# Fetching the first two tables of the second block's short transform one step earlier in the program

## The chip, the cores and the metric

The kernel runs on one core of a Trainium2 chip. The metric is the device time of one execution in microseconds (us). Beside it stands the profile of one execution: every instruction of the five engines (PE for matrix products, ACT for exponentials, DVE for element-wise work, POOL, which here mostly issues transfers, and SP, which issues the other transfers), and the transfers themselves.

## The reference

Two unrelated results are put side by side: an attention layer with 32 query heads and one shared key and value head, and a long causal convolution.

```python
# half A: x is (1, 2048, 512), 32 heads of 16, one key and one value head
q = (x @ wq).reshape(B, S, 32, 16).transpose(0, 2, 1, 3)
k, v = x @ wk, x @ wv
p = softmax(einsum("bhqd,bkd->bhqk", q, k) * 16 ** -0.5)
a = einsum("bhqk,bkd->bhqd", p, v).transpose(0, 2, 1, 3).reshape(B, S, 512) @ wo

# half B: q, k, v are (1, 2048, 512)
k_shift = sum(shift(k, i) * shift_k[:, i] for i in range(4))   # four taps along the sequence
kv = k_shift * v
y = irfft(rfft(pad(kv)) * rfft(pad(ssm_k)))[:2048] + kv * ssm_D
b = q * y

out = concatenate([a, b], axis=-1)                             # (1, 2048, 1024)
```

## The kernel before

**Attention is the backbone.** The scores of 16 stacks of queries against 16 tiles of keys are computed tile by tile. For each tile PE makes 8 products into a pair of PSUM banks (`keys`, L1092), ACT takes the exponential of 128 x 1024 elements (`exp`, L1110), and PE multiplies the result with the values (`pv`, L1134). The scores have two such bank pairs, so the scores of a tile wait for the exponential of the tile two before.

**The convolution fills what is left.** Half B is done in two blocks of 256 channels, as transforms made of products with tables of cosines and sines (PE, `halves`, L274) and a 16-point transform on DVE. A block has these parts:

- the *short* transform (`short_forward`): the element-wise product `a` of the four taps and `v`, for 128 x 2 x 256 elements in each of eight groups (`m2` = 0 to 7), is multiplied with the table `ff` of its group;
- the *long* transform (`long_forward`): the same with the convolution's kernel;
- the product of the two spectra and the inverse 16-point transform, both on DVE;
- the *inverse* transform (`backward`): eight groups, each with a table `fi` and a slice of `q`; DVE multiplies the outcome with `q` into `r` (L490), and POOL sends `r` to the output (L492).

**Tables.** `table` (L316 to L320) allocates one of four rotating buffers (tag `ft`) for a table of 128 x 2 x 2 x 128 numbers and issues two transfers of 128 KB for it on POOL's queue. The `ff` and the `fi` tables share these four buffers. `short_forward` fetches the tables of its groups 0 and 1 when it begins, and the table of group `m2 + 1` in each later step. `paced` makes a transfer wait for the exponential that was issued two tiles before.

**Order.** The order of all instructions is fixed when the program is built. Python generators ("threads") stand for the parts; at each tile `_Fill.turn` asks each thread in turn for work and lets it emit as much as a budget allows. Each engine then runs what was emitted for it in that order, and waits at an instruction until the semaphores it needs are set. Two threads matter here. `conv_pe` runs, for the place of the change, `backward(0)` and then `short(1)`, which calls `short_forward(1, ...)`. `conv_short` runs `short_products(1, ...)`, which makes the `a` of the second block on DVE and issues, for each group, the transfers of the `kk` rows two groups ahead (L398) and of `v` (L411) on POOL. It may begin when `backward(0)` has reached its group 7, where `("b", 0)` is added to `self.seen`.

**POOL's queue is in order.** A transfer that waits there holds up every transfer behind it. Each transfer issued on POOL uses one of eight semaphores in turn (DMASW0 to DMASW7), and waits until the transfer that used the same one before, eight transfers earlier, has landed.

The first product of group 0 of the second block waits for its table's first transfer and for `a` of group 0:

```python
y = self.nc.tensor.matmul(out[j : j + 32, cols], w[r, j : j + 32], x[r], ...)   # L274, w is the table, x is a
```

Of the kernel before, what the change touches and what calls it, by code (L numbers as in the profile page):

```python
# [111 lines left out]
class _Emit:  # L112
# [203 lines left out]
    def table(self, n, m2):  # L316
# [2 lines left out]
            self.paced(self.nc.gpsimd.dma_start(t[:, i], self.I[n][:, 2 * m2 + i]))  # L319
        return t  # L320

    def s2(self, n, shape=(2, CB), dt=F32):
        return self.w.tile([P, *shape], dt, tag="s2", bufs=S2, name=self.nm(n))

# [109 lines left out]

    def short_forward(self, blk, cx):

        ft = {i: self.table("ff", i) for i in range(2)}
        for m2 in range(8):
            yield from self.after(("a", blk, m2))
            if 2 <= m2 + 1 < 8:  # L440
                ft[m2 + 1] = self.table("ff", m2 + 1)
            yield from self.forward(self.kv2[m2], cx, 2 * m2, ft[m2])
            self.seen.add(("x", blk, m2))
# [15 lines left out]
    def backward(self, blk):  # L459

        nc, w = self.nc, self.w
        cs = slice(blk * CB, (blk + 1) * CB)
        ft, q = {i: self.table("fi", i) for i in range(2)}, {}

        def load(m2):
            if m2 > 1:
                ft[m2] = self.table("fi", m2)
            q[m2] = self.s2("q")
            for i in range(2):
                self.paced(nc.gpsimd.dma_start(q[m2][:, i], self.qr[:, 2 * m2 + i, cs]))  # L470

        load(0)
        load(1)
        yield WAIT, 4
        yield from self.after(("y", blk))
        cx, (g1, g2) = self.sp["y", blk]
        for m2 in range(8):
            if m2 < 6:
                load(m2 + 2)
            if m2 == 7:  # L480
                self.seen.add(("b", blk))
            r = self.s2("r")
            cols, work = slice(0, CB), [[], []]
            for i in range(2):
                m = 2 * m2 + i
                for cc in range(2):
                    x = cx[:, cc, 4 * g2[m // 4] + g1[m % 4], :]
                    work[i].append((cols, ft[m2][:, i, cc, :], x))
            b = yield from self.halves(*work, 2, 850)
            nc.vector.tensor_tensor(r, self.both[:, :, cols], q[m2], ALU.mult)  # L490
            for i in range(2):
                nc.gpsimd.dma_start(self.orr[:, 2 * m2 + i, D + blk * CB : D + (blk + 1) * CB], r[:, i])  # L492
# [1153 lines left out]
```

## Time and profile before

| | |
|---|---|
| time, median of 3 runs | 983.58 us (983.55 to 984.63) |
| the profiled execution's own time | 983.59 us |
| its span, first to last instruction | 981.7 us |
| PE busy / ACT busy / DVE busy / POOL busy | 95% / 97% / 76% / 18% of the span |
| mean granted clock of PE | 0.998 |
| chain that ended last | PE 49%, ACT 35%, issue 7%, DVE 6%, DMA 2% |

The span is what the profile covers; the time has 1.89 us more around it. Busy shares are means over stages; the waits and the rows in order of time tell which engine holds up which at a place.

### The profile page before, as it was taken

The numbers are of one execution on the slowest core, as the hardware profiler recorded it, in microseconds if no ns is written. First come the engines' busy times: TensorE is split into PE (matmuls) and PEld (weight loads), VectorE is DVE, ScalarE is ACT, GpSimd is POOL, SyncE is SP. The second block draws the span as 40 slices with busy tenths as digits, with TensorE's granted clock in tenths as the row PEclk, the third lists the DMA queues.
The fourth block names the chain that finished last, engine by engine and source line by source line (L and its number), as shares of the span: only waits on it lengthen the run. The fifth ranks groups of instructions, "written<-read, shape, count | busy, mean of one in ns | idle before, by whom it ended". The sixth has DMA issues, their size and how long they took to land.

```text
span 981.7 us, 51442 instructions
## 1 busy us (share of the span) xinstructions
PE 934.5 (95%) x23570; PEld 462.4 (47%) x23570; DVE 748.9 (76%) x932; ACT 951.2 (97%) x1032; POOL 173.3 (18%) x321
## 2 busy tenths in 40 slices
PE   8999999989999999999899899999988999999996
PEld 5344454435444444444444455444434444444453
DVE  4647785988369989998996578799889927876753
ACT  5999999999999999999999999999999999999994
POOL 5240231321030001110533432000000132100000
PEclk9999999999999999999999999999999999999999
DMA  7252432431133212211443233011121232112101
GB/s 253 74 172 81 141 118 73 105 105 56 35 91 85 87 55 89 84 55 49 146 130 109 90 117 97 22 55 44 54 83 56 65 119 83 60 56 76 49 11 48
DMA packets 69205, 82.93 MB, mean 84 GB/s; under 512 B 20752, under 2 KB 58294, under 8 KB 68982
## 3 DMA queue, kind: packets, MB, share of 16 engines
q1 hardware_dynamic: 47558, 43.48, 14.1%
q0 software_dynamic: 20320, 35.46, 12.2%
q8 instruction: 186, 3.05, 1.3%
q10 hardware_dynamic: 1104, 0.64, 0.2%
q14 instruction: 37, 0.30, 0.1%
HBM read 54.46 MB, written 25.03 MB: 81 GB/s over the span
## 4 chain that ended last, share of the span: by engine, by line
PE 49%; ACT 35%; issue 7%; DVE 6%; DMA 2%; SPq 0%; POOL 0%; ACTq 0%; DVEq 0%
ACT p L1110 34%; PE f L1134 22%; PE s L1092 15%; PE f L274 10%; DVE sp L189 1%; DMA r<-rd 1%; DVE sp L193 1%; DMA xa<-in_A_x 1%; DVE sp L457 0%; DMA ff<-in_ff 0%; PE f L663 0%; DVE o L1278 0%; PE f L255 0%; PE f L693 0%; DVE ao L1143 0%
## 5 line engine op out<-in xcount | busy, mean ns | idle before, releaser
L1110 ACT ACTIVATE p<-s 128x1024 f32<-128x1024 f32 x1008 | 929.8, 1068 | 6.6 <-PE s L1092 5.1
L1134 PE MATMUL f<-p,vx 64*32 64x512 f32 (+1 forms) x8832 | 544.3, 552 | 0.4 <-ACT p L1110 0.2
L1092 PE MATMUL s<-st,kst 49*32 49x512 f16 x8128 | 422.5, 380 | 31.6 <-ACT p L1110 27.8
L1092 PEld LDWEIGHTS <-kst 49*32 49x32 f16 x8192 | 199.3, 89 | 395.3 <-issue 347.7
L1134 PEld LDWEIGHTS f<-p,vx 64*32 64x32 f32 x8832 | 175.0, 106 | 26.0 <-issue 3.0
L314 DVE COPY sp<-f 128x1024 f32<-128x1024 f32 x32 | 39.1, 1222 | 62.6 <-PE f L274 62.6
L189 DVE TENSOR_TENSOR sp<-sp 128x2048 f32<-128x2048 f32 x35 | 80.0, 2287 | 0.9
L319 POOL DMA_DIRECT2D ff<-in_ff x64 | 35.3, 557 | 235.3 <-ACT p L1110 216.9
L274 PE MATMUL f<-wo,o 64*32 64x512 f16 x1440 | 56.6, 375 | 0.9 <-DVE wp L1330 0.5
L1143 DVE COPY ao<-f 128x512 f32<-128x512 f32 (+1 forms) x33 | 22.2, 674 | 40.5 <-PE f L1134 40.2
L274 PE MATMUL f<-xT,wq 64*32 64x512 f16 x1344 | 51.0, 375 | 0.0
L319 POOL DMA_DIRECT2D fi<-in_fi x32 | 17.5, 552 | 176.5 <-ACT p L1110 176.3
L189 DVE TENSOR_TENSOR sp<-sp,sp 128x2048 f32<-128x2048 f32 x19 | 43.4, 2286 | 0.5
L274 PE MATMUL f<-a,ff 64*32 64x256 f32 x1024 | 41.2, 377 | 1.4 <-DMA ff<-in_ff 1.4
L274 PE MATMUL f<-hT,ff 64*32 64x256 f32 x1024 | 40.8, 377 | 0.7 <-DVE hT L368 0.7
L274 PE MATMUL f<-sp,fi 64*32 64x256 f32 x1024 | 39.9, 375 | 0.0
L492 POOL DMA_DIRECT2D out<-r x32 | 17.3, 546 | 123.8 <-DVE r L490 112.4
L429 DVE TENSOR_TENSOR a<-a,t 128x512 f32<-128x512 f32 x48 | 33.1, 690 | 1.5
L420 DVE TENSOR_TENSOR t<-kk,tpb 128x512 f32<-128x512 f32 (+1 forms) x50 | 33.0, 663 | 0.0
L347 POOL DMA_DIRECT2D hin<-in_B_ssm_k x32 | 21.1, 662 | 60.0 <-ACT p L1110 58.5
L193 DVE TENSOR_TENSOR sp<-sp 128x1024 f32<-128x1024 f32 x26 | 30.8, 1215 | 0.0
L490 DVE TENSOR_TENSOR r<-f,q 128x512 f32<-128x512 f32 x16 | 11.0, 688 | 25.4 <-PE f L274 25.3
(197 smaller groups left out, 788.3 us busy)
## 6 DMA issues: line engine op xcount, KB each, us to landing
ff<-in_ff POOLq DMA_DIRECT2D x64, 128.0 KB, 2.9
od<-ao SPq DMA_DIRECT2D x60, 128.0 KB
qd<-qp SPq DMA_DIRECT2D x48, 128.0 KB
st<-qd SPq DMA_DIRECT2D x62, 98.0 KB
kk<-in_B_k POOLq DMA_DIRECT2D x32, 128.0 KB, 2.8
v<-in_B_v POOLq DMA_DIRECT2D x32, 128.0 KB, 2.7
hin<-in_B_ssm_k POOLq DMA_DIRECT2D x32, 128.0 KB, 5.6
fi<-in_fi POOLq DMA_DIRECT2D x32, 128.0 KB, 2.9
```

What stands on the lines that cost most here:

```text
L189: v.tensor_tensor(out, a, b, op)
L193: v.tensor_tensor(part(out), part(a), part(b), op)
L274: y = self.nc.tensor.matmul(out[j : j + 32, cols], w[r, j : j + 32], x[r], start=half == m == 0, stop=half == 1 and m == k - 1,)
L314: self.nc.vector.tensor_copy(out, self.both.rearrange("p i (q n) -> p i q n", q=2))
L319: self.paced(self.nc.gpsimd.dma_start(t[:, i], self.I[n][:, 2 * m2 + i]))
L347: self.paced(nc.gpsimd.dma_start(dst, src))
L420: nc.vector.tensor_tensor(out[:, n], kk[:, x], tap(i, n.stop - n.start), ALU.mult)
L429: nc.vector.tensor_tensor(a, a, t, ALU.add)
L1092: self.nc.tensor.matmul(s[j : j + 32, e, :], (self.kst[k * P] if k * P in self.kst else self.kst[k * P - P][:, P:CB])[rows, j : j + 32], s ...
L1110: self.exps[u % 4] = self.nc.scalar.activation(self.pt[u], s, AF.Exp, scale=LN2 * DH**-0.5 / SC / SC)
L1134: nc.tensor.matmul(self.acc[e][32 * j : 32 * j + 32, m], vx[rows, :], y, start=k == 0, stop=stop)
L1143: nc.vector.tensor_copy(a, self.acc[0][:, m])
```

## The change

`backward`, when it reaches group 7 of block 0, now also allocates and fetches the tables of groups 0 and 1 of the second block's short transform, and `short_forward` of block 1 takes them from there. For block 0 nothing is changed.

```diff
+    def first_tables(self):
+        return {i: self.table("ff", i) for i in range(2)}
+
     def short_forward(self, blk, cx):
 
-        ft = {i: self.table("ff", i) for i in range(2)}
+        ft = self.next_ft if blk else self.first_tables()
         for m2 in range(8):
             yield from self.after(("a", blk, m2))
...
     def backward(self, blk):
...
             if m2 == 7:
                 self.seen.add(("b", blk))
+                self.next_ft = self.first_tables() if blk == 0 else None
             r = self.s2("r")
```

The order on POOL at the end of block 0's inverse transform, before the change. `out<-r` are the transfers of groups 5, 6 and 7 of `backward(0)` (the third is group 7's), `kk` and `v` are loads of the second block for DVE, and the two `ff` are the tables of groups 0 and 1:

```order
L492 DMA out<-r_12243 128x256 x2
L492 DMA out<-r_12437 128x256 x2
L398 DMA kk_10955<-in_B_k 128x256 x2
L411 DMA v_12673<-in_B_v 128x256 x2
L492 DMA out<-r_12670 128x256 x2
L319 DMA ff_12842<-in_ff 128x256 x2
L319 DMA ff_12845<-in_ff 128x256 x2
L398 DMA kk_10955<-in_B_k 128x256 x2
L411 DMA v_12904<-in_B_v 128x256 x2
```

The same place in the changed program (its line numbers are 3 or 4 higher from `first_tables` on):

```order
L496 DMA out<-r_12243 128x256 x2
L496 DMA out<-r_12437 128x256 x2
L319 DMA ff_12670<-in_ff 128x256 x2
L319 DMA ff_12673<-in_ff 128x256 x2
L401 DMA kk_10955<-in_B_k 128x256 x2
L414 DMA v_12679<-in_B_v 128x256 x2
L496 DMA out<-r_12676 128x256 x2
L401 DMA kk_10955<-in_B_k 128x256 x2
L414 DMA v_12904<-in_B_v 128x256 x2
```

The four table transfers moved ahead of six others: `kk` and `v` of group 0's step and the last `out<-r`. These are the only transfers on POOL that change places.

With their waits, the transfers behind group 6's `out<-r` were, before (`Activation` is the pacing exponential, `PE` the last reader of the buffer, DMASWn the transfer eight places earlier):

```order
L398 DMA kk_10955<-in_B_k 128x256 [waits DMASW6_49,Activation_49]
L398 DMA kk_10955<-in_B_k 128x256 [waits DMASW7_49]
L411 DMA v_12673<-in_B_v 128x256 [waits DMASW0_49]
L411 DMA v_12673<-in_B_v 128x256 [waits DMASW1_49]
L492 DMA out<-r_12670 128x256 [waits DMASW2_49,DVE_49]
```

and are now:

```order
L319 DMA ff_12670<-in_ff 128x256 [waits DMASW6_49,Activation_49]
L319 DMA ff_12670<-in_ff 128x256 [waits DMASW7_49]
L319 DMA ff_12673<-in_ff 128x256 [waits DMASW0_49,PE_49]
L319 DMA ff_12673<-in_ff 128x256 [waits DMASW1_49]
L401 DMA kk_10955<-in_B_k 128x256 [waits DMASW2_49]
L401 DMA kk_10955<-in_B_k 128x256 [waits DMASW3_49]
L414 DMA v_12679<-in_B_v 128x256 [waits DMASW4_49]
L414 DMA v_12679<-in_B_v 128x256 [waits DMASW5_49]
L496 DMA out<-r_12676 128x256 [waits DMASW6_49,DVE_49]
```

The wait for the pacing exponential moved from `kk` to the first `ff`, the second `ff` waits for PE's last reading of its buffer, and `v` now waits for the landing of group 6's `out<-r` (DMASW4 and DMASW5). On PE, ACT, DVE and SP every instruction stands where it stood.

## The prediction

> **What bounds the kernel now.** I read the page first, then the wait table, then the rows in order of time around the place of the change. From the page:
>
> ```profile
> span 981.7 us, 51442 instructions
> PE 934.5 (95%) x23570; PEld 462.4 (47%) x23570; DVE 748.9 (76%) x932; ACT 951.2 (97%) x1032; POOL 173.3 (18%) x321
> L1110 ACT ACTIVATE p<-s 128x1024 f32<-128x1024 f32 x1008 | 929.8, 1068 | 6.6 <-PE s L1092 5.1
> L274 PE MATMUL f<-a,ff 64*32 64x256 f32 x1024 | 41.2, 377 | 1.4 <-DMA ff<-in_ff 1.4
> ```
>
> ACT and PE are both full, and the exponentials of L1110 stood idle for only 6.6 us in all. The last row is the place of this change: in 1024 products with `ff` tables and data `a`, PE waited for a table once, for 1.4 us. The wait table for 552 to 562 us shows that this one wait reaches ACT:
>
> ```profile
> PE f L274 <- DMA ff<-in_ff: 1.4, 1, 1.4
> ACT p L1110 <- PE s L1092: 1.4, 1, 1.4
> DVE a L431 <- DMA v<-in_B_v: 0.7, 1, 0.7
> ```
>
> The chain of waits runs through the same transfer (start, length, what):
>
> ```profile
> 551.18 0.70 DVE r L490
> 552.17 0.47 POOL out L492
> 552.71 0.54 POOL out L492
> 553.24 4.17 DMA ff<-in_ff
> 557.54 0.67 PE f L274 x9
> ```
>
> So the table issued at 553.24 landed at 557.41 (553.24 + 4.17), and PE began with it at 557.54. It was issued late because POOL stood before it in group 7's `out<-r`, which waits for `r` of 551.18. ACT around it:
>
> ```profile
> 539.76 17.58 ACT L1110 ACTIVATE p<-s 128x1024 f32<-128x1024 f32 x19
> 558.75 185.11 ACT L1110 ACTIVATE p<-s 128x1024 f32<-128x1024 f32 x201 [1.41 <-PE s L1092]
> 559.82 1.94 ACT L1110 ACTIVATE p<-s 128x1024 f32<-128x1024 f32 x2
> ```
>
> Nineteen exponentials ran without a gap, then a gap of 1.41 us, then 201 without a gap: ACT is the limit on both sides of the hole.
>
> **The change, part by part.** *The hole that goes.* Of the 19 exponentials the last takes 1.07 us (the 1068 ns of the group), so the others follow each other every (17.58 - 1.07) / 18 = 0.917 us. The next would have begun at 539.76 + 19 x 0.917 = 557.19; it began at 558.75, 1.56 us late. The one after it began 1.07 us behind, at 559.82, another 0.15 us over the beat: 1.71 us late. The gap alone is 1.41 us. These are the lower and the upper bound, 1.41 and 1.71; I take **1.6 us**, between the 1.56 of the first exponential and the 1.71 that the second has lost.
>
> *Can PE fill it?* PE's rows:
>
> ```profile
> 545.48 0.41 PE L1092 MATMUL s<-st,kst 49*32 49x512 f16 x8
> 545.69 1.06 PE L1134 MATMUL f<-p,vx 64*32 64x512 f32 x16
> 547.31 0.41 PE L1092 MATMUL s<-st,kst 49*32 49x512 f16 x8
> 554.64 0.41 PE L1092 MATMUL s<-st,kst 49*32 49x512 f16 x8 [0.35 <-ACT p L1110]
> 555.72 0.41 PE L1092 MATMUL s<-st,kst 49*32 49x512 f16 x8
> 557.54 0.67 PE L274 MATMUL f<-a,ff 64*32 64x256 f32 x12 [1.41 <-DMA ff<-in_ff]
> ```
>
> Behind 8 score products the next work starts 0.21 us later (545.48 to 545.69), so with its table there the product of 557.54 could start at 555.93, 1.61 us earlier. With filler in it a pair of tiles took PE 1.83 us (545.48 to 547.31), which is twice ACT's 0.917, so PE keeps the beat with these products among its others. The products also need `a`:
>
> ```profile
> 533.53 0.68 DVE L490 TENSOR_TENSOR r<-f,q 128x512 f32<-128x512 f32 x1
> 546.38 0.75 DVE L420 TENSOR_TENSOR t<-kk,tpb 128x256 f32<-128x256 f32 x2
> 553.83 0.69 DVE L431 TENSOR_TENSOR a<-a,v 128x512 f32<-128x512 f32 x1
> 559.88 0.69 DVE L431 TENSOR_TENSOR a<-a,v 128x512 f32<-128x512 f32 x1 [0.70 <-DMA v<-in_B_v]
> 570.50 0.63 PE L274 MATMUL f<-a,ff 64*32 64x256 f32 x16
> ```
>
> `a` of group 0 is finished at 554.52 (553.83 + 0.69), 1.41 us before 555.93. It is the latest input left, and it doesn't bind.
>
> *What moves on POOL.* Its rows, and the spread from issue to landing of the four `ff` (3.6 to 4.2) and of the `out<-r` (2.0 to 3.0):
>
> ```profile
> 544.83 1.07 POOL L492 DMA_DIRECT2D out<-r  x2 [9.24 <-DVE r L490]
> 545.90 1.08 POOL L398 DMA_DIRECT2D kk<-in_B_k  x2
> 546.97 1.07 POOL L411 DMA_DIRECT2D v<-in_B_v  x2
> 552.17 1.08 POOL L492 DMA_DIRECT2D out<-r  x2 [4.13 <-DVE r L490]
> 553.24 2.13 POOL L319 DMA_DIRECT2D ff<-in_ff  x4
> 555.37 1.07 POOL L398 DMA_DIRECT2D kk<-in_B_k  x2
> 556.43 1.07 POOL L411 DMA_DIRECT2D v<-in_B_v  x2
> DMA to landing us min/median/max: 3.6/3.9/4.2
> DMA to landing us min/median/max: 2.0/2.8/3.0
> ```
>
> The `ff` take the place at 545.90. Their two added waits are met there: the pacing exponential is the one that `kk` waited for, and `kk` went at 545.90 without idling; the buffer of the second table was last read for group 5's `r`, which DVE made at 533.53. The four issues take 2.13 us, so `kk` goes at 548.03, `v` from 549.10 to 550.17. Before 552.17 POOL idled 4.13 us, which covers the 2.13; without that cover group 7's `out<-r` would go 2.13 us later, and nobody on DVE or PE waits for that. From 553.24 on the queue is 2.13 us ahead.
>
> *Who waits for the delayed `v`.* DVE at 553.83, and behind it PE. The trace has the same ten transfers in one go, two `out<-r`, four `ff`, two `kk`, two `v`, from 552.17 on; there `v` was in by 559.88, since DVE waited for it until then, 7.71 us after the first issue. From 544.83 the same train has the tables in by 550.07 (557.41 - 552.17 = 5.24 later) and `v` by 552.54: 5.9 us before PE could use the tables, 1.3 us before DVE needs `v`. `v`'s new wait, for the two `out<-r` issued from 544.83, ends for the first by 547.83 (3.0 us later), before 549.10, and for the second, issued 0.54 us after it, by 548.37, before 549.64. The cost of all this is nothing, with 1.3 us of cover for `v`, and 2.7 us until PE waits (1.3 + 1.41).
>
> *What else it brings.* `kk` and `v` of the next step go 2.13 us earlier, and DVE's wait of 0.70 us at 559.88 goes. PE needs that `a` at 570.50 only, ten microseconds later, so it is worth nothing; if it were on the path after all, the gain would be 1.6 + 0.7 = 2.3 us.
>
> *The sum.* 983.59 (the profiled execution) - 1.6 = **982.0 us**, bounds 981.9 and 982.2. The median of the runs is 983.58, so it is the same against that.
>
> [...] From 552 to 556 us DVE (third figure after the comma) was busy for 3.90 of 4.00 us, and POOL (fifth) for 3.83:
>
> ```profile
> 552.00:556.00 4.00, 3.31 (x80) 1.25 (x67) 3.90 (x8) 4.00 (x5) 3.83 (x8) 1.00 0.52 156
> ```
>
> POOL's eight issues from 553.24 on still took 0.53 us each. [...]
>
> **The rivals.** *The gap comes back later, nothing gained: 983.6 us.* Something that doesn't move with PE and ACT would have to take the 1.6 us. For it: the chain of waits goes through transfers later on, as the first row shows. Against it: the 201 exponentials from 558.75 run to 743.86 (558.75 + 185.11) without a gap, and DVE has idled for PE before and in between (the other rows), so what follows hangs on the same beat:
>
> ```profile
> 725.22 4.07 DMA r<-rd
> 574.92 1.23 DVE L314 COPY sp<-f 128x1024 f32<-128x1024 f32 x1 [3.86 <-PE f L274]
> 710.46 0.69 DVE L1143 COPY ao<-f 128x512 f32<-128x512 f32 x1 [2.21 <-PE f L1134]
> ```
>
> *Slower, `v` takes the table's place as the late input.* `v` of group 0 now stands behind the tables. If it lands after 555.24 (555.93 - 0.69) PE waits for `a`, and from 556.85 (557.54 - 0.69) on it loses. Issued last at 549.64, it would have to take 7.2 us. At twice the longest landing seen here, 8.4 us, it lands at 558.04, PE starts at 558.73, 1.2 us later than before: **984.8 us**. Against it: the train from 552.17 had it in 1.3 us early by its measure.
>
> *The early fetch isn't early.* If pacing or the buffers held POOL until group 7's products end (`r` begins at 551.18), the four `ff` would go from 551.2 and the tables land 4.2 us later, at 555.4, still before 555.93. But `v` would go at 554.4 and 554.9 and land 2.8 us later, the median there, at 557.7, and `a` be ready at 558.4:
>
> ```profile
> v<-in_B_v POOLq DMA_DIRECT2D x2, 128.0 KB, 2.8
> ```
>
> PE would start 0.9 us later than at 557.54: 984.5 us. Against it: the reader is group 5, not 7, and `kk`, paced alike, went at 545.90.
>
> *More than the hole.* With the 0.7 us of DVE, 2.3 us: **981.3 us**. PE's late use of that `a` speaks against it.
>
> **How the numbers follow.** The forecast has 0.74, within 0.3 us of 982.0 by its bounds and some half a microsecond for the scatter of the runs; nothing gained or a good part lost again 0.10; more than the hole 0.10; slower or no earlier 0.06. The runs of before lie 983.55 to 984.63, so about 0.2%, 2 us, is what can be told from no change. A gain of 1.6 us is 0.16%, just below that line: the likeliest verdict is "no change" although the hole goes. Faster by over 0.2% needs 981.6 or less: the case of more than the hole, and a share of the forecast by scatter, 0.20 together. Slower by over 0.2% needs 985.5: 0.04, from a `v` that takes longer still. The rest, 0.76, is the same. The range, 981.2 to 983.6, goes from "more than the hole" to "nothing gained"; the slower cases and larger gains are left out of it.
>
> **What would show it.** Right: in the profile after, `ff` on POOL at about 546 and `kk`, `v` 2.1 us behind their old places; no wait of PE for `ff` around 556; the exponential of 558.75 at about 557.2 and no gap there; the end of that run of exponentials and the last instruction 1.6 us earlier; a span near 980.1. Wrong: a gap of ACT at 556 to 558 that ends with `a` or `v`; a first `ff` on POOL that waits; or that exponential at 557.2 and a span that has not shrunk, with a larger wait after the run of exponentials.

## The result, and the profile after

The two kernels were timed side by side on one chip.

| | before | after |
|---|---|---|
| time, median | 984.75 us (22 runs, 982.88 to 987.85) | 983.20 us (22 runs, 979.87 to 984.90) |
| ratio | | 0.9982, 95% interval 0.9973 to 0.9990 |
| the profiled execution's own time | 983.59 us | 983.52 us |
| its span | 981.7 us | 981.8 us |
| its mean granted clock of PE | 0.998 | 0.996 |

By the ratio the change saves 1.8 us of 984.75, with 1.0 to 2.7 us as its interval (0.0018, 0.0010 and 0.0027 times 984.75). The ratio is not the quotient of the two medians, which is 0.9984, or 1.55 us. The interval leaves out 1, so the gain is real; it is just below the 0.2% that the prediction counts as a change. The runs of either kernel spread over about 5 us, and the three runs shown of before lay lower than its median in this comparison. The profiled executions alone would say that nothing was gained, since their spans agree. From the page of the kernel after:

```profile
span 981.8 us, 51442 instructions
PE 936.5 (95%) x23570; PEld 462.8 (47%) x23570; DVE 749.1 (76%) x932; ACT 951.2 (97%) x1032; POOL 172.9 (18%) x321
L1114 ACT ACTIVATE p<-s 128x1024 f32<-128x1024 f32 x1008 | 929.7, 1069 | 6.5 <-PE s L1096 5.1
```

PE was busy 2.0 us longer with the same 23570 products (936.5 against 934.5), and the exponentials (now L1114) lost as much time to PE as before. So the place of the change has to be read by itself. The wait table of after for 552 to 562 us:

```profile
PEld L1096 <- issue: 4.6, 16, 0.7
DVE r L494 <- PE f L274: 4.0, 1, 4.0
POOL out L496 <- DVE r L494: 2.0, 1, 2.0
PE s L1096 <- ACT p L1114: 0.7, 2, 0.3
```

PE's 1.4 us for `ff`, ACT's 1.4 us behind it and DVE's 0.7 us for `v` are all gone; PE now waits for ACT instead. Where the gain went is told by the rows of the exponentials in order of time, over 180 to 820 us. Before:

```profile
179.45 30.42 ACT L1110 ACTIVATE p<-s 128x1024 f32<-128x1024 f32 x33
210.61 89.47 ACT L1110 ACTIVATE p<-s 128x1024 f32<-128x1024 f32 x97 [0.74 <-PE s L1092]
300.62 256.72 ACT L1110 ACTIVATE p<-s 128x1024 f32<-128x1024 f32 x279 [0.54 <-PE s L1092]
744.09 27.05 ACT L1110 ACTIVATE p<-s 128x1024 f32<-128x1024 f32 x29 [0.24 <-PE s L1092]
```

After:

```profile
179.79 30.43 ACT L1114 ACTIVATE p<-s 128x1024 f32<-128x1024 f32 x33
211.62 1.02 ACT L1114 ACTIVATE p<-s 128x1024 f32<-128x1024 f32 x1 [1.39 <-PE s L1096]
213.49 88.40 ACT L1114 ACTIVATE p<-s 128x1024 f32<-128x1024 f32 x96 [0.85 <-PE s L1096]
302.44 441.59 ACT L1114 ACTIVATE p<-s 128x1024 f32<-128x1024 f32 x480 [0.55 <-PE s L1096]
744.18 27.05 ACT L1114 ACTIVATE p<-s 128x1024 f32<-128x1024 f32 x29 [0.16 <-PE s L1096]
```

The counts let us compare equal work. 33 + 97 = 130 exponentials lie before the row at 300.62, and 33 + 1 + 96 = 130 before the row at 302.44. Before then runs 279 exponentials, the hole, and the 201 of the row at 558.75; after runs 279 + 201 = 480 in one row, with no hole in it. From there to the start of the next row, the 611th exponential counted from 180 us on in both, it is 744.09 - 300.62 = 443.47 us before and 744.18 - 302.44 = 441.74 us after, 1.73 us less. Of these, 0.08 us are not the hole's: the gap just ahead of that exponential was 0.24 us before and 0.16 after. Without it, **the hole was worth 1.65 us, and it is gone**. The execution of after had started the stretch 302.44 - 300.62 = 1.82 us late. Of these, 0.34 us were there at 180 us; the other 1.48 us came between 180 and 302 us, before anything in the program differs. The windows of after show what they are (the columns are length, then busy time and count of PE, weight loads, DVE, ACT and POOL, then the granted clock):

```profile
206.14:209.55 3.41, 1.89 (x44) 0.56 (x31) 2.36 (x6) 3.41 (x5) 1.06 (x2) 1.00 0.13 35
209.55:212.96 3.41, 3.41 (x48) 1.66 (x56) 3.38 (x8) 1.70 (x2) 0.00 (x0) 0.50 0.58 169
```

For 3.41 us PE was granted half its clock, and the 34th and 35th exponential had to wait for their scores (1.39 and 0.85 us, where before had 0.74). By chance the execution of before that was shown has no such fall. The two things cancel in the spans.

POOL after, and the spread from issue to landing of the four `ff`:

```profile
546.66 1.07 POOL L496 DMA_DIRECT2D out<-r  x2 [9.24 <-DVE r L494]
547.72 2.13 POOL L319 DMA_DIRECT2D ff<-in_ff  x4
549.84 1.06 POOL L401 DMA_DIRECT2D kk<-in_B_k  x2
550.89 1.06 POOL L414 DMA_DIRECT2D v<-in_B_v  x2
554.00 1.08 POOL L496 DMA_DIRECT2D out<-r  x2 [2.04 <-DVE r L494]
DMA to landing us min/median/max: 2.5/2.8/3.0
```

The `ff` went without waiting, the others 2.13 us behind them, and POOL still had 2.04 us to spare ahead of group 7's `out<-r`. The use of the tables on PE, and DVE's product with `v` before it:

```profile
557.76 0.63 PE L274 MATMUL f<-a,ff 64*32 64x256 f32 x16
555.66 0.69 DVE L434 TENSOR_TENSOR a<-a,v 128x512 f32<-128x512 f32 x1
561.04 0.69 DVE L434 TENSOR_TENSOR a<-a,v 128x512 f32<-128x512 f32 x1
```

All 16 products start with no wait, and neither product of DVE waits for `v`.

### The profile page after: what moved, and what is told of

Read it like the earlier page. It is cut to its first block, busy times and chain, and to the rows that moved or that the text cites. A ratio compares the mean times of both kernels' runs of the same rounds, so it can differ in the third digit from the quotient of the medians.

```text
span 981.8 us, 51442 instructions
## 1 busy us (share of the span) xinstructions
PE 936.5 (95%) x23570; PEld 462.8 (47%) x23570; DVE 749.1 (76%) x932; ACT 951.2 (97%) x1032; POOL 172.9 (18%) x321
## 4 chain that ended last, share of the span: by engine, by line
PE 50%; ACT 35%; issue 7%; DVE 5%; DMA 2%; SPq 0%; ACTq 0%; DVEq 0%
ACT p L1114 34%; PE f L1138 23%; PE s L1096 15%; PE f L274 10%; DVE sp L189 1%; DMA r<-rd 1%; DVE sp L193 1%; DMA xa<-in_A_x 1%; DVE sp L460 0%; PE f L667 0%; PE x L630 0%; DVE o L1282 0%; PE f L255 0%; PE f L697 0%; PE f L630 0%
## 5 line engine op out<-in xcount | busy, mean ns | idle before, releaser
L1114 ACT ACTIVATE p<-s 128x1024 f32<-128x1024 f32 x1008 | 929.7, 1069 | 6.5 <-PE s L1096 5.1
```

The lines of the kernel that those rows point to most:

```text
L1114: self.exps[u % 4] = self.nc.scalar.activation(self.pt[u], s, AF.Exp, scale=LN2 * DH**-0.5 / SC / SC)
```

## The experiments

**One table alone.** The first product needs group 0's table only. If the hole is the late table, the first table early brings the whole gain and the second table early brings none. A rival is that the gain is shared between them, or comes from the `kk` and `v` that go earlier afterwards.

First table alone:

```diff
-        ft = self.next_ft if blk else self.first_tables()
+        ft = {**self.next_ft, 1: self.table("ff", 1)} if blk else self.first_tables()
...
-                self.next_ft = self.first_tables() if blk == 0 else None
+                self.next_ft = {0: self.table("ff", 0)} if blk == 0 else None
```

> Only the table of group 0 is fetched at group 7 of the inverse transform, the table of group 1 where it was before. Theory (PE waits for the table of group 0 alone; the table of group 1 is first needed some 13 us later): the whole gain is kept, 1.6 us below the kernel before, no wait of PE for ff near 556 us. Rival (what helps is that kk and v of the next step go 2.1 us earlier): half of it, since they go only 1.07 us earlier: 0.8 us below. Rival (the two equal spans of 981.7 and 981.8 are the truth and nothing is gained): 0.0.

Measured: 983.2 us against 985.37 for the kernel before on that chip, ratio 0.9979 (0.9969 to 0.9988), the same as with both tables. From its exponentials and its wait table for 548 to 566 us:

```profile
303.12 468.19 ACT L1114 ACTIVATE p<-s 128x1024 f32<-128x1024 f32 x509 [0.88 <-PE s L1096]
DVE a L434 <- DMA v<-in_B_v: 0.2, 1, 0.2
```

The exponentials run through the place of the hole in a row of 509. The whole gain is in the first table.

Second table alone (as above with 0 and 1 exchanged):

> Only the table of group 1 is fetched early; the table of group 0 is issued behind group 7's output as before. Theory: the wait of PE stays, shorter only by what the table lands sooner with two transfers fewer beside it (3.6 us, the shortest landing seen there, for 4.2): 0 to 0.6 us below the kernel before, a gap of ACT of 0.8 to 1.4 us. Rival (earlier kk and v): 0.8 us below. Rival (nothing matters): 0.0.

Measured: 984.45 us on the same chip, ratio 1.0000 (0.9989 to 1.0010). Its waits, its exponentials and its `ff`:

```profile
PE f L274 <- DMA ff<-in_ff: 1.7, 1, 1.7
301.28 256.71 ACT L1114 ACTIVATE p<-s 128x1024 f32<-128x1024 f32 x279 [0.65 <-PE s L1096]
559.56 211.71 ACT L1114 ACTIVATE p<-s 128x1024 f32<-128x1024 f32 x230 [1.56 <-PE s L1096]
DMA to landing us min/median/max: 2.8/3.6/4.5
```

No gain is seen, although `kk` and `v` of the next step went 1.07 us earlier, two issues fewer standing before them. The interval by itself would still hold the 0.8 us of that rival (a ratio of 0.9992). The trace does not: from the exponential near 301 us to the one behind the hole, the same 279 later, it took 559.56 - 301.28 = 258.28 us here and 558.75 - 300.62 = 258.13 us in the kernel before. The size was missed: the hole was expected smaller, with two transfers fewer beside the late table, and it was 1.56 us. The late table landed no sooner for it.

**Later still.** In the kernel before, the two tables were moved behind `kk` and `v` of the next step, so that they are later by these four issues:

```diff
-        ft = {i: self.table("ff", i) for i in range(2)}
+        ft = {} if blk else {i: self.table("ff", i) for i in range(2)}
...
             yield from self.after(("a", blk, m2))
+            if m2 not in ft:
+                ft.update({i: self.table("ff", i) for i in range(2)})
```

> The kernel before with the four table transfers put behind kk and v of group 1's step, 2.13 us later than before. Theory: the table lands 1.5 to 2.1 us later, ACT's gap grows from 1.41 to 2.9 to 3.5 us, and the kernel is 1.5 to 2.1 us slower than the kernel before; PE then idles over 3 us in one piece, and the granted clock may fall to 0.5 behind it for some 3.4 us, as it did at 209.6 us in the profile of the changed kernel, which would add about 1.5 us more. Rival (earlier kk and v help): faster than before by up to 0.7 us, since kk and v go 2.13 us earlier here too. Rival (nothing matters): 0.0.

Measured: 987.23 us, ratio 1.0020 (1.0009 to 1.0030), 2.0 us slower (0.0020 times 985.37). From its wait table, its exponentials and its windows:

```profile
PE f L274 <- DMA ff<-in_ff: 3.0, 1, 3.0
561.90 1.03 ACT L1112 ACTIVATE p<-s 128x1024 f32<-128x1024 f32 x1 [3.61 <-PE s L1094]
563.85 210.61 ACT L1112 ACTIVATE p<-s 128x1024 f32<-128x1024 f32 x229 [0.92 <-PE s L1094]
556.60:560.00 3.40, 0.48 (x16) 0.02 (x7) 3.30 (x6) 1.69 (x2) 1.84 (x4) 1.00 0.74 230
560.00:563.41 3.41, 3.37 (x48) 2.23 (x56) 0.82 (x2) 1.03 (x1) 0.00 (x0) 0.50 0.01 2
```

The dose works: a table issued 2.1 us later makes a larger hole. But it grew from 1.41 to 3.61 + 0.92 us, more than 2.1, because the clock fell right behind the hole, after 3.40 us in which PE was busy for only 0.48. In its eight runs the mean clock was never above 0.996, while nine of the 26 runs of before on that chip had 0.998 or 0.999. A fall of 3.41 us at half clock lowers the mean by 3.41 x 0.5 / 982 = 0.0017. The profiled executions of before and after also end at half clock, for their last 4.8 and 4.2 us, which lowers the mean by 0.0025 and 0.0021. By an estimate from these, that alone doesn't bring it to 0.996, so each run of this kernel had at least one fall.

**Where on POOL the tables go.** Two places other than the one chosen. Behind `v` of group 0, just ahead of group 7's `out<-r`, so that `kk` and `v` aren't delayed (`kv_products` of the second block calls `first_tables` behind its `v`):

```diff
+            if m2 == 0 and blk:
+                self.next_ft = self.first_tables()
```

> The changed kernel with the four table transfers behind v of group 0 and ahead of group 7's output, so that kk and v keep their old places. Theory (only the tables were late; v had over a microsecond to spare): the same as the changed kernel, 1.6 us below the kernel before, no gap near 556 us. Rival (moving v back costs something in the changed kernel): faster than the changed kernel by up to 0.7 us.

And one group earlier, in group 6 of the inverse transform:

```diff
-            if m2 == 7:
-                self.next_ft = self.first_tables() if blk == 0 else None
+            if m2 == 6:
+                self.next_ft = self.first_tables() if blk == 0 else None
```

> The changed kernel with the fetch one group earlier, at group 6 of the inverse transform, about 10 us sooner. Theory (once the tables are there before PE comes to them, sooner brings nothing): the same as the changed kernel, 1.6 us below the kernel before. Rival (the tables of the changed kernel still land too late in some executions): up to 0.5 us below the changed kernel. Rival (the buffers or the pacing hold POOL): a wait of the first ff on POOL and a later output of group 6, no gain.

Measured: 982.07 us, ratio 0.9975 (0.9960 to 0.9991), and 983.31 us, ratio 0.9980 (0.9967 to 0.9992), both against 984.77 on their chip. The exponentials of the first, then of the second:

```profile
301.24 468.59 ACT L1115 ACTIVATE p<-s 128x1024 f32<-128x1024 f32 x509 [0.94 <-PE s L1097]
```

```profile
300.97 441.71 ACT L1115 ACTIVATE p<-s 128x1024 f32<-128x1024 f32 x480 [0.64 <-PE s L1097]
744.10 1.02 ACT L1115 ACTIVATE p<-s 128x1024 f32<-128x1024 f32 x1 [1.42 <-PE s L1097]
```

Neither has a hole at 556 to 558 us. (The second has a gap of 1.42 us for ACT at 744 us, and a mean clock of 0.996, so by the estimate above a fall somewhere.) The interval of each holds the ratio of the change. So each of the three places that has the first table in before PE needs it takes the hole away, and the times can't be told apart: that sooner brings more, or that the delay of `kk` and `v` in the change costs something, does not show.

**The hole without a change.** Two further executions of the unchanged kernel were profiled, to see how constant the hole is.

> The kernel before, unchanged, for another profile of the hole. In three profiles of programs with the table of group 0 in its old place, ACT stood still for 1.41, 1.56 and 0.4 us there, and the table landed 2.4 to 4.5 us after its issue. Theory (the hole is the lateness of the landing, and that differs between executions): 0.4 to 1.9 us, tied to the landing. Rival (the hole is fixed, the 0.4 belongs to the added score tiles of that run): 1.3 to 1.6 us.

> The same kernel once more, with the same expectations: a hole of 0.4 to 1.9 us tied to the table's landing by the theory, 1.3 to 1.6 us whatever the landing by the rival.

The exponential behind the hole, and the spread of the `ff` from issue to landing, in the first:

```profile
560.33 211.70 ACT L1110 ACTIVATE p<-s 128x1024 f32<-128x1024 f32 x230 [1.55 <-PE s L1092]
DMA to landing us min/median/max: 3.7/4.0/4.5
```

and in the second:

```profile
211.00 346.06 ACT L1110 ACTIVATE p<-s 128x1024 f32<-128x1024 f32 x376 [0.73 <-PE s L1092]
558.40 212.29 ACT L1110 ACTIVATE p<-s 128x1024 f32<-128x1024 f32 x230 [1.33 <-PE s L1092]
DMA to landing us min/median/max: 3.5/3.8/4.1
```

The hole is 1.33 to 1.55 us. Both expectations hold these values, so the two executions alone don't decide between them. But the order is that of the landing: the slowest of the four `ff` took 4.1, 4.2 and 4.5 us in the second, in before and in the first, and the gap was 1.33, 1.41 and 1.55 us. Their single times, 984.05 and 982.61 us, differ for another reason too: the first has a mean clock of 0.996 and gaps of 1.23 and 1.11 us around one exponential at 211.49 us, like those of after at its fall (1.39 and 0.85), the second has 0.999 and a single gap of 0.73 us there. The gap near 300 us, 0.5 us in the profiles of before and after, is in neither: the second has 376 exponentials in one row there, and the first 375, from 213.62 us on.

**Fillers for PE.** The window before the fall in after holds only 44 products in 3.41 us. The next theory was that PE's thin work there lets its clock fall, and that filling it would keep the clock. Five score tiles between 204 and 210 us were made again, three of them once and two twice, which is 56 added products (they go to the same place, so the output stays as it is), in the kernel after and in the kernel before:

```diff
+FILL = {191: 1, 193: 1, 194: 1, 195: 2, 196: 2}
...
+        for _ in range(FILL.get(u, 0)):
+            self.keys(s, n, k, a, cols)
```

> The changed kernel with seven score tiles around 203 to 209 us made twice or three times by PE (the same products again, overwritten), so that PE is busier in the thin stretch ahead of 209.6 us. Theory (a thin stretch of 3.4 us lets the granted clock fall to 0.5 for the next 3.4 us in some executions, which costs about 1.5 to 1.8 us): no execution with a mean clock of 0.996 is left, the median lies 0.8 to 1.5 us below the changed kernel and 2.4 to 3.2 us below the kernel before, and the scatter shrinks. Rival (the fall of the clock has nothing to do with how busy PE is): as the changed kernel, 1.6 us below the kernel before, or slower by the 1.5 us of the added products if PE has no room.

> The kernel before with the same seven added score tiles at 203 to 209 us as in the run of the changed kernel with them. Theory (the added products and the early tables act apart): it keeps the hole of 1.4 to 1.6 us near 557 us and lies 1.6 us above that run and about 3.5 us below the kernel before; if the hole too lets the clock fall in some executions, some of its executions have a mean clock of 0.996 or 0.997 and its scatter is wider than there. Rival (the early tables gain only through the clock, not by the hole): no difference to that run in executions without a fall of the clock.

Measured: the changed kernel with fillers 979.84 us, ratio 0.9950 (0.9937 to 0.9963) to the kernel before on its chip; the kernel before with fillers 981.3 us, ratio 0.9959 (0.9944 to 0.9974) on another. The first gains 3.4 us on the kernel with the first table early, 983.2 us on the same chip, which is more than the 1.48 us of one fall. The same window, and its exponentials:

```profile
206.20:209.60 3.40, 2.96 (x84) 1.11 (x72) 2.38 (x6) 3.19 (x5) 1.06 (x2) 1.00 0.18 47
210.99 610.04 ACT L1117 ACTIVATE p<-s 128x1024 f32<-128x1024 f32 x663 [0.38 <-PE s L1099]
```

PE is busy for 2.96 us instead of 1.89, no fall follows (the clock is 1.00 from 209.60 to 213.01 us), and 663 exponentials run to the end of the window without a gap. The gaps near 300, 744 and 771 us are gone too, which no theory had expected of fillers at 204 us.

The kernel before with fillers has its tables in the old place, issued from 553.33 us on. Its `ff`, its exponentials around the place, DVE's product with `v`, and PE's wait behind that:

```profile
DMA to landing us min/median/max: 2.4/2.7/2.8
549.01 16.99 ACT L1113 ACTIVATE p<-s 128x1024 f32<-128x1024 f32 x18
566.39 3.78 ACT L1113 ACTIVATE p<-s 128x1024 f32<-128x1024 f32 x4 [0.39 <-PE s L1095]
561.77 0.69 DVE L432 TENSOR_TENSOR a<-a,v 128x512 f32<-128x512 f32 x1 [2.51 <-DMA v<-in_B_v]
564.97 1.09 PE f L1137 x16
```

In this execution the tables landed in 2.4 to 2.8 us instead of 3.6 to 4.2, and the hole is not there: 18 exponentials in 16.99 us, 0.3 us over the beat of 0.917 us that the prediction used (16.99 - 1.07 - 17 x 0.917). Instead `v` was late: DVE waited 2.51 us for it, its next copies were late, PE's products (the chain's piece at 564.97) came after them, and ACT idled 0.39 us at 566 us. The expectation was missed: a hole of 1.4 to 1.6 us was to stay, and this kernel was to be 1.6 us above the changed one with fillers. By the ratios it is 0.0009, or 0.9 us, above it, and the intervals overlap. So with fillers the runs don't show what the early tables still bring. How much of the gain of this kernel's seven runs is the fillers' and how much a hole that was not there, one profile can't say.

To see whether it is the filled window that counts, seven repeated tiles were put elsewhere in the kernel after: some 8 us earlier, between 196 and 202 us (`FILL = {181: 1, ..., 187: 1}`), at 729 to 741 us (`FILL = {759: 1, 761: 1, ..., 771: 1}`), and at both the first and the last place.

> The changed kernel with the same number of added products, 56, but in seven tiles of 194 to 201 us, 8 us ahead of the thin stretch of 206 to 209.6 us. Theory (the clock falls after a thin stretch of one period of 3.41 us): the falls at 209 us stay, the executions split between mean clocks of 0.996 and 0.998 as in the changed kernel, and the time is that of the changed kernel to within 0.7 us (the gap of 0.5 to 0.9 us near 300 us, which was gone with the fill, may go here too if it hangs on where PE's instructions lie in the program). Rival (any added products ahead of 209 us do it, for instance by the place of the instructions): as the run with the fill at 203 to 209 us, 3 us below the changed kernel.

> The changed kernel with 56 added products in seven score tiles at about 729 to 741 us, behind everything at 209 and 300 us. Theory A (added products help through the clock): a fall of the clock at 209 us stays, one at 741 us as in the run with the fetch at group 6 goes: 0 to 0.5 us below the changed kernel, mean clocks of 0.996 remain. Theory B (the extra gain of the three fills came from the place of PE's later instructions in the program): the gap of 0.7 to 1.1 us at the 293rd exponential, near 300 us, stays, since the instructions ahead of it are as before, and gaps between 742 and 779 us go; 1 us below the changed kernel. Rival (any 56 added products bring it): 2.5 us below the changed kernel and no gap near 300 us.

> The changed kernel with the fill at 203 to 209 us and the fill at 729 to 741 us. Theory A: no fall of the clock at either place, so the median is that of the run with the first fill alone or up to 0.3 us below it, some 5 us below the kernel before, with mean clocks of 0.997 and above only. Theory B: the later instructions of PE lie 112 rows further on once more, and a gap of 0.3 to 0.7 us can come back behind 742 us. Rival (the gain of the first fill was the chip's or the day's): 2 us below the kernel before.

| fillers in the kernel after | time | ratio to before |
|---|---|---|
| none | 983.20 us | 0.9982 (0.9973 to 0.9990) |
| at 204 to 210 us | 979.84 us | 0.9950 (0.9937 to 0.9963) |
| at 196 to 202 us | 980.57 us | 0.9951 (0.9934 to 0.9968) |
| at 729 to 741 us | 981.92 us | 0.9968 (0.9955 to 0.9981) |
| at 204 to 210 and at 729 to 741 us | 982.02 us | 0.9971 (0.9956 to 0.9985) |

The times come from different chips, so the ratios are compared (the kernel before had medians of 985.37, 984.77 and 984.82 us on the three of the experiments). The early fillers leave the thin stretch thin (by the windows PE was busy for 1.49 + 0.82 us of the four from 206 to 210 us, against 1.59 + 0.90 in after) and brought as much as those in it, so the theory of that stretch doesn't hold as it was put. And both places together brought no more than the late one, 2.9 us below the kernel before by the ratio, where fillers that act through the clock were to bring some 5. The late fillers lie 1.4 us below the change by the ratios; the clock alone was to bring 0 to 0.5, and any 56 products 2.5. Their profiled execution took 985.5 us and is the slowest of their twelve, the others lying at 980.56 to 982.75, so its gaps are not typical of them. The exponentials, of the early fillers, of the late ones, and of both:

```profile
211.52 608.94 ACT L1117 ACTIVATE p<-s 128x1024 f32<-128x1024 f32 x662 [0.74 <-PE s L1099]
```

```profile
304.91 468.60 ACT L1117 ACTIVATE p<-s 128x1024 f32<-128x1024 f32 x509 [1.15 <-PE s L1099]
```

```profile
195.05 16.27 ACT L1117 ACTIVATE p<-s 128x1024 f32<-128x1024 f32 x17 [0.55 <-PE s L1099]
304.48 475.26 ACT L1117 ACTIVATE p<-s 128x1024 f32<-128x1024 f32 x516 [0.57 <-PE s L1099]
780.65 39.69 ACT L1117 ACTIVATE p<-s 128x1024 f32<-128x1024 f32 x43 [0.92 <-PE s L1099]
```

With both fillers the gaps at 195, 304 and 780 us are back. The gap near 300 us is 0.54 us in before, 0.55 in after and 1.15 with late fillers. It is absent in both further executions of the kernel before, and in three of the four kernels that have fillers ahead of it. It is PE that is late there each time, and the same instructions are sometimes on time. **What stays open**: what makes PE late by 0.2 to 1.2 us near 300 us and from 740 to 780 us in some executions, and so how much of the 1 to 3 us of the fillers is theirs. No run here settles it. The mean clocks of the runs show about how much of the fillers' gain can be the clock's. Of the 22 runs of the changed kernel, nine had a mean of 0.996, so by the estimate above at least one fall each, and five more had 0.997, which may hide one. Of the twelve runs with fillers at 204 to 210 us (five of the changed kernel, seven of the kernel before) none was below 0.997. At 1.48 us a fall, nine to fourteen falls in 22 runs are an estimated 0.6 to 0.9 us a run, not the 3.2 us by which the fillers in the changed kernel lie below the change by the ratios.

The changed kernel with fillers at 204 to 210 us has the lowest ratio, with that of the early fillers right beside it, and its interval, from five runs, lies below that of the change.

## Why the prediction was right, and where it was off

**What bounds the kernel, and the hole.** Right. PE's one wait for `ff` was the hole, one late table caused it, and the exponentials on both sides hang on ACT's beat. Moving the first table alone took the hole away, moving the second alone left it, moving both later enlarged it.

**The hole's size.** Forecast 1.6 us, between 1.41 and 1.71; measured 1.65 us in the traces and 1.8 us (1.0 to 2.7) in the times. The step "between the 1.56 of the first exponential and the 1.71 that the second has lost" held; the gap of 1.41 alone was too little. Two single traces differ in small gaps elsewhere, so the last 0.1 us can't be read from them, and in other executions of the kernel before the gap itself was 1.33 and 1.55 us.

**PE can fill it.** Right: the product forecast for 555.93 started at 557.76, in an execution that was 1.82 us late: 557.76 - 1.82 = 555.94. `a` was made from 555.66 on, which is 553.84 on that scale, against 553.83 before: it moved by nothing and did not bind.

**POOL and `v`.** Right in what happened, too good in the margin. The first `ff` waited for nothing, `kk` and `v` came 2.13 us later, and `out<-r` of group 7 still waited for DVE. Of the train, the forecast had only the landing of its first `ff` (the 4.17 us that PE waited for), and its "tables in by 550.07" is that transfer and not all four. On the scale of this execution 5.24 us behind the first issue is 546.66 + 5.24 = 551.9. The first `ff`, issued at 547.72, was in by 550.7 at the latest (3.0 us later), and the last, issued at 549.32 (547.72 + 2.13 - 0.53), by 552.3. For `v` the forecast was too good: on this scale it was to be in by 546.66 + 7.71 = 554.4. Its second transfer, issued at 551.42, landed 3.5 to 3.8 us later, the range of the four `v` there, at 554.9 to 555.2, and DVE used it at 555.66. So 0.4 to 0.7 us of the 1.3 us of cover were left. It was enough, and DVE did not wait, but with the 4.62 us that `v` took in the kernel before with fillers DVE would have waited.

**DVE's 0.7 us are worth nothing.** They went, and the gain is the hole without them, so it holds here. As a general statement it fails at larger sizes: when `v` came 2.51 us late, with the tables in the old place, 0.39 us reached ACT. The way there was not the forecast's `a` and its products at 570 us but DVE's order: the copies queued behind the waiting product, for which PE waits sooner.

**The issues and landings beside DVE's products.** The four issues of `ff` that moved under DVE's products, from 547.72 on, took 0.53 us each (2.13 for four), as in the old place, and the tables landed in 2.5 to 3.0 us, sooner than the 3.6 to 4.2 there. So no delay by DVE's products shows here.

**The rivals.** "The gap comes back later": the exponential at 744 us still had the whole gain of the hole. "`v` takes the table's place" and "the early fetch isn't early": the rows of POOL and DVE show neither. "More than the hole", 2.3 us, is inside the interval of the times; by the traces it is not what happened.

**The span near 980.1.** Wrong: it was 981.8. The step that failed is the one that turned one trace into another, "a span near 980.1", as if two executions differed only by the change. The one profiled after had a clock fall worth 1.48 us that the one before had not.

**The level and the scatter.** The time came out 1.2 us above 982.0, and inside the range of 981.2 to 983.6. It is outside the 0.3 us and half a microsecond to which the forecast gave its 0.74, and 0.4 us from the range's end, "nothing gained". That the number still lay inside is luck. The gain was right; the level was not, because the three runs shown of before (983.55 to 984.63) were taken for its whole scatter, "some half a microsecond". With 22 runs the kernel before had a median of 984.75, 1.17 us above the 983.58 of the three runs, and spread over 5 us. The mis-sized term is this half a microsecond.

## What to carry to other kernels

Where an engine that others wait for stops once for one transfer, read the gain of fetching it earlier from the hole in the beat of the bounding engine. Here that hole went as soon as the transfer landed ahead of the need, and fetching still sooner added nothing that could be measured. Compare two traces at equal work, by counting instructions of the bounding engine, not by their spans: here equal spans hid the whole gain. Before a forecast of 0.2% is stated as a time, the scatter of the runs is worth more attention than the second decimal of the hole.

## What the runs showed of the hardware

**PE's clock fell in the middle of a busy kernel.** Pieces of 3.41 us at half clock stand in the windows of after (209.55 to 212.96 us), of the first table alone (210.00 to 213.41) and behind the enlarged hole (560.00 to 563.41); those of before have none ahead of its end. The profiled executions with the tables one group earlier, with late fillers and of the first further look at before also have a mean clock of 0.996, so by the estimate above a fall each. The one in after cost 1.48 us, nearly as much as the whole change. The 3.41 us before it had 44 products and 1.89 us of PE work.

In the clock records of before and after, half clock begins on a grid of such pieces. In after the fall lasts 3.413 us and begins 204.80 us after PE's first moment at full speed, and the half clock at the end begins 972.80 us after that moment, in before as in after. That is 60 and 285 times 3.4133 us. PE was not idle ahead of the fall in after: it was busy for 1.89 of the 3.41 us. Ahead of the fall at 560 us it was busy for only 0.48 us of 3.40.

Where the grid lies differs between executions: the first moment at full speed lay at 4.10 us in before and at 4.75 in after. The piece of after's grid ahead of its fall held 1.89 us of PE work, and the 3.40 us ahead of the fall with the first table alone held 1.89 too; the thinnest piece of before's grid at this place, from 205.49 to 208.90 us, held 2.15 us, and no fall came. Split over two pieces of its grid, before had a stretch as thin, 1.89 us of PE work from 206.20 to 209.60. But how busy PE is in 3.41 us does not decide by itself. None followed 2.13 us ahead of the hole in before, or 1.69 us at the hole with the second table alone:

```profile
553.65:557.06 3.41, 2.13 (x48) 0.73 (x39) 3.34 (x7) 3.41 (x5) 3.41 (x8) 1.00 0.72 213
556.34:559.75 3.41, 1.69 (x56) 1.09 (x48) 3.31 (x6) 1.84 (x3) 0.75 (x2) 1.00 0.50 155
```

So the falls seen in the windows came behind thin stretches, not behind every one. Where the stretch lies on the grid may matter; what decides is not shown, and no run here set the grid on purpose.

**The time from issue to landing changed between executions.** The four `ff` in the old place took 3.6 to 4.2, 3.7 to 4.5 and 3.5 to 4.1 us in three executions of the kernel before, and 2.4 to 2.8 with fillers, where the hole vanished and `v` was late in its place. A hole that hangs on one landing is therefore itself a matter of the execution, and a forecast from one trace carries that uncertainty.
